# Transposing x of two more blocks by DMA, and a planner that expects later landings

## The chip, the cores and the metric

The kernel runs on one core of one Trainium2 chip. The metric is the device time of one execution in microseconds; the median of six runs of the kernel before is 218.59 us (218.05 to 218.89).

## The reference

Attention with a band and a few global keys, and behind it a two-layer feed-forward network with softplus. B = 4 batches, H = 8 heads, S = 768 positions, D = 64; the band holds the 96 positions up to the query, and the first 8 keys of a batch are seen by all queries.

```
scores = q @ k.T / sqrt(D) + bias            # bias = -slope of the head * distance
a      = softmax(where(local or global, scores, -1e9))
x      = (a @ v), heads side by side: 3072 tokens x 512
h      = x @ w_in                             # 512 x 2048
out    = softplus(h) @ w_out                  # 2048 x 512, float32
```

## The kernel before

**Tiling.** The 3072 tokens are 24 blocks of 128, six per batch. Loads of q, k and v come in windows of two blocks (12 windows, number w; block n belongs to window n // 2). The feed-forward network works in groups of 256 tokens, so group g needs blocks 2g and 2g + 1 and no others.

**A block of attention**, in two halves of four heads: scores on TensorE (L488) into one of two PSUM tiles s_ps; for blocks 4 and later VectorE adds the bias and writes z (L519); ScalarE takes the exponential and writes the probabilities pb (L525); TensorE multiplies them with v into the PSUM tile x_ps, of which there is one (P·V, L540 and L543), where a column of ones gives the sum of each row; VectorE takes the reciprocal (L554) and writes the normalized x as xs in bf16 (L555). The second half's P·V waits until that has emptied x_ps. A block needs its own keys and values and those of the block before it in its batch; small copies put the global keys and values in (L457 on GpSimd, L466 on VectorE).

**x transposed.** The feed-forward network wants x with features on the partitions, in the tile XT. There are two ways, chosen by the constant X_DMA. Blocks below it: four PE transposes against the identity (x_transp, L565) into a PSUM bank and one copy by VectorE or ScalarE (x_out, L574). Blocks from it on: one DMA transpose of 128x512 issued by SP (x_dma, L577).

**q and k transposed.** Windows below T_DMA = 4 go through TensorE. From window 4 on, q is cast to bf16 by VectorE (L388), k by GpSimd in four pieces (L397), and SP issues two DMA transposes for each (L436). v is cast by GpSimd too (L397, four pieces).

**The feed-forward network.** A unit of the first layer is eight matmuls (mm1, L587) into one of two PSUM banks h_ps; ScalarE takes exp (L598) and, for two units at once, log(1 + e) (L606). There are eight units to a group and twelve groups. The second layer (mm2, L615, and L640 for the last group) accumulates in o_ps, for group 0 in s_ps; VectorE copies it out (L659) and SP stores it (L664).

**What sets the order.** Every engine runs its instructions in the order in which they were emitted. This order comes from a planner (class Planner), which simulates the engines while the program is built: each operation has a duration, operations that it comes after, buffers that it takes and frees, and a rank. An engine that is free takes, of the operations that can start, the one of lowest rank. Ranks come from the block or group, from BASE (a number per block, for the first 14 blocks) and from RANKS (a correction for one operation by its name: pv51.0 is the P·V of block 5, second half). For DMAs the planner keeps a model of the queues; an operation with slack is held to be done that much later than its modelled landing (`self.at(op.end + op.slack, ...)`), which touches the plan and no instruction. When TensorE has nothing to do in the first 24 us of the plan, a filler matmul on zeros is emitted (L727).

**Loads.** All loads of q, k and v are issued by SP in one chain; the weights are issued by GpSimd. A load named in HALVED is issued as two DMAs of four heads each; the cast that follows waits for both.

Of the kernel before, what the change touches and what calls it, by code (L numbers as in the profile page):

```python
# [14 lines left out]


RANKS = {
    "Ck3.0": 26.1, "biasA.0": -5.4, "castv1.1": 16.6, "mm1_1_7.0": -3.8, "mm1_1_6.0": -1.5,
    "mm1_1_4.0": 19.1, "bias71.0": 48.3, "mm2_1_7.0": -15.1, "pv51.0": 12.5, "pv60.0": -32.7,
    "mm2_1_3.0": -38.9, "mm1_0_2.0": 5.1, "mm2_1_5.0": 4.5, "bias20.0": 20.2, "castv4.2": 18.4,  # L20
    "mm1_0_7.0": 13.1, "castv4.0": -15.4, "TX0.0": -16.5, "bias30.0": 6.3, "mm2_1_1.0": 13.7,
    "scores7.0": 10.3, "pv10.0": 15.2, "mm1_2_3.0": -4.2, "mm2_0_3.0": 15.3, "mm1_0_3.0": 18.1,
    "castv4.1": 7.7, "mm1_2_4.0": -12.6, "bias01.0": -7.6, "castv0.3": -1.4, "norm11.0": -4.2,
    "castv0.6": -4.6, "exp61.0": -5.6, "scores50.0": -15.4, "castv3.3": -1.5, "mm2_0_1.0": 16.5,
    "castv2.1": -4.7, "norm20.0": 5.2, "castk5.3": 11.8, "castk4.1": -4.2, "castv0.0": 5.4,
    "mm1_0_4.0": 9.3, "Fq1.0": -2.3, "norm10.0": 6.1, "castv0.5": -0.8, "castv2.2": -0.7,
    "castv3.0": -2.8, "bias0.1": -5.2, "castv1.0": 0.2, "castv3.2": -0.4, "Fk3out.0": -10.8,
    "TX5.0": -6.6,
}
HALVED = "q9 k9 q10 k10 v10 q11 k11 v11".split()  # L30
EARLY, MERGED, T_DMA, X_DMA = 4, 6, 4, 6
SP_ORDER = "Q01 K01 v0a Q23 K23 v0b v1 q2@in1 k2 v2 q3@in2 k3 v3"
POOL_ORDER = "in0@Q23 in1 out0 out1@q2 in2 in3 out2 out3"
BASE = (-29.92, -34.26, -30.09, -12.77, -7.13, 15.38, 14.34, -22.2, 17.37, 24.12, 29.7, 32.51, 31.67, 35.31)


class Op:
# [202 lines left out]
def kernel(  # L240
# [101 lines left out]
    def load(w, what, heads=slice(0, H), key=None, waits=()):  # L342
        b, ww = divmod(w, WPB)
        src = {"q": q, "k": k, "v": v}[what][b, heads, W * ww : W * ww + W, :]
        dst = raw_of(what, w)[:, heads, :]
        send(key, nc.sync.dma_start(dst, src.rearrange("h (p r) d -> p h (r d)", r=2)), waits)  # L346
# [38 lines left out]
    def cast(eng, w, what, hs=slice(0, H)):  # L385
        src = raw_of(what, w)
        t = tile_of(qkv, (what + "b", w), [P, 2, H, D], BF16)
        copy_on[eng](t[:, :, hs, :], src[:, hs, :].rearrange("p h (r d) -> p r h d", r=2))  # L388

    def cast_by_block(eng, w, what, blk, r, hs=slice(0, H)):  # L390

        if what == "v":
            dst = vb_ring[w % NRING][:, blk, :, 0:D]
        else:
            dst = tile_of(qkv, (what + "b", w), [P, 2, H, D], BF16)[:, blk, :, :]
        src = raw_of(what, w)[64 * blk : 64 * blk + 64, hs, r * D : r * D + D]
        copy_on[eng](dst[64 * r : 64 * r + 64, hs, :], src)  # L397

    def tr_bank(taken):
        return bank_of(taken[-1]).bitcast(BF16)  # L400
# [33 lines left out]
    def transp_dma(w, what, i):  # L434
        dst = q_tile(w) if what == "q" else k_tile(w)
        nc.sync.dma_start_transpose(  # L436
            dst[:, i, :, :], state[what + "b", w][:, i, :, :].rearrange("p h d -> p (h d)")
        )
# [265 lines left out]
    bias0 = const.tile([P, 2, 4, P], BF16, name="bias0")  # L704
    biasA = const.tile([P, 2, 8, P], BF16, name="biasA")
# [36 lines left out]
    def base(n):  # L742
        return BASE[n] if n < len(BASE) else 4.0 * n - 13.0

# [4 lines left out]
    def add_load(w, what, rank, after=(), hs=ALL, key=None, waits=()):  # L749
        nonlocal chain  # L750
        f = 0.5 if hs != ALL else 1.0
        dur, dma = 0.55 * f + 0.05, (64 * f, 28)
        takes = ((what + "32",),) if hs.start == 0 else ()
        o = chain = pl.add(
            f"load{what}{w}", "sp", dur, lambda op: load(w, what, hs, key, waits), rank,
            after=[*after, *(landed[x] for x in waits)], behind=[chain], takes=takes, dma=dma,
        )
        loaded.setdefault((w, what), []).append(o)
        return o
# [13 lines left out]
    def load_rest(w, rank, after=()):  # L773
        for i, what in enumerate("qkv"):
            for hs, _ in halves if what + str(w) in HALVED else whole:
                add_load(w, what, rank + 0.01 * i, after, hs)
# [85 lines left out]
    def attention_window(w):  # L862
# [7 lines left out]
        for part, (hs, ms) in enumerate(whole if w >= 2 else ()):  # L870
            f = len(ms) / NPAIR
            for what in "qk":
                if w < 4:
                    eng = {"pool": 1.05 * f, "act": 0.2 + 0.85 * f, "dve": 0.1 + 0.6 * f}
                else:
                    eng = {"dve": 0.69} if what == "q" else {"pool": 1.05}
                if what == "k" and w >= T_DMA:
                    c = [
                        pl.add(
                            f"castk{w}", {"pool": 0.68}, 0,  # L880
                            lambda op, blk=blk, r=r: cast_by_block(op.on, w, "k", blk, r),
                            u - 7.93 + 0.01 * blk, after=loaded[w, "k"],
                            takes=(("kb",),) if blk == r == 0 else (),
                        )
                        for blk in range(2) for r in range(2)
                    ]
                    for x in c[1:]:
                        x.behind.append(c[0])
                        x.left += 1
                    pl.add(  # L890
                        f"k{w}", "none", 0.0, lambda op: None, -999.0, after=c,
                        frees=[(loaded[w, "k"][0], "k32")],
                    )
                    casts[w, "k", 0] = c[0]
                else:
                    c = casts[w, what, part] = pl.add(
                        f"cast{what}{w}", eng, 0,
                        lambda op, what=what, hs=hs: cast(op.on, w, what, hs),
                        u - (7.94 if w < T_DMA else 5.33) + 0.1 * (what == "k"),
                        after=loaded[w, what],  # L900
                        takes=((what + "b",),),
                        frees=[(loaded[w, what][0], what + "32")],
                    )
                    c = [c]
                wait = [*c, *(done if what == "k" else ())]
                takes = (("qT",),) if what == "q" else ()
                free_b = [(casts[w, what, 0], what + "b")]
                r = u + (-3.8 if what == "q" else -2.3)
                if w >= T_DMA:
                    for i in range(2):  # L910
                        o = pl.add(
                            f"D{what}{w}", "sp", 1.3,
                            lambda op, what=what, i=i: transp_dma(w, what, i), u - 14.96,
                            after=wait if what == "q" else [*c[2 * i : 2 * i + 2], *done],
                            takes=takes if i == 0 else (), dma=(32, 27), slack=1.2,
                            frees=free_b if i else (),
                        )
                        outs.setdefault((w, what, 0), []).append(o)
                        if i == 0:
                            first_t[w, what] = o  # L920
                    continue
                t = pl.add(
                    f"T{what}{w}", "pe", 0.45 * f,
                    lambda op, what=what, ms=ms: transp(w, what, tr_bank(op.taken), ms),
                    r, after=wait, takes=(*takes, TR),
                )
                first_t[w, what] = t
                o = pl.add(
                    f"T{what}{w}out", {"dve": 0.28 + 0.42 * f, "act": 0.2 + 0.8 * f}, 0,
                    lambda op, t=t, what=what, ms=ms: transp_out(  # L930
                        op.on, w, what, tr_bank(t.taken), ms
                    ),
                    r + 0.1, after=[t], frees=[(t, TR_ALL), *free_b],
                )
                outs[w, what, part] = [o]
        split = w < 2 and f"v{w}a" in landed
        for part, (hs, _) in enumerate(halves if split else whole):
            f = 0.5 if split else 1.0
# [134 lines left out]
    for w in range(NWIN):  # L1073
        attention_window(w)
        for n in (2 * w, 2 * w + 1):
            attention_block(n)

    mm1s, mm2s, lns, copies = {}, {}, {}, {}
    for g in range(NGRP):
# [18 lines left out]
        if g == NGRP - 1:  # L1098
            before = None
            for part, (ns, cols, _) in enumerate(LAST):  # L1100
                f = (cols.stop - cols.start) / DM
# [97 lines left out]
```

## Time and profile before

| | |
|---|---|
| median of six runs | 218.59 us |
| the profiled execution | 218.67 us |
| its span, first to last instruction | 216.9 us |
| TensorE matmul (PE) busy | 208.7 us, 96% |
| ScalarE (ACT) busy | 154.2 us, 71% |
| VectorE (DVE) busy | 121.7 us, 56% |
| GpSimd (POOL) busy | 58.0 us, 27% |
| DMA queue of SP, share of 16 engines | 60.3% |
| L587 matmuls, first layer | 768, 95.9 us busy |
| L615 matmuls, second layer | 295 recorded, 75.3 us busy |
| L565 PE transposes of x | 24 (20 into h_ps, 4 into o_ps) |
| L577 DMA transposes of x | 18, median 3.0 us from issue to landing |
| granted TensorE clock | 1.000 |

Busy times of matmuls overlap, because they are pipelined: four transposes of 219 ns each take 0.39 us together. Starts are recorded and ends are modelled, so a distance from start to start is the safer measure of what one costs. The page cuts the span into 40 slices of 5.4 us; a digit is the busy share in tenths. In the lists of time, "idle before" in square brackets is the time that the engine stood before an instruction, and the name behind the arrow is what it waited for. PEld is the loading of weights into TensorE, which runs beside the matmuls. Some matmul records are missing.

### The profile page before, as it was taken

To read this page: it belongs to the slowest core of one execution; us is meant where nothing else is said; L and a number is where in the kernel's file an instruction comes from. 1 tells how busy PE (TensorE), PEld (TensorE's weight loads), DVE (VectorE), ACT (ScalarE), POOL (GpSimd) and SP (SyncE) were. 2 spreads that over 40 slices of the span, in tenths; PEclk is the share of its full clock that TensorE was granted. 3 is DMA by queue.
4 is the path that set the end of the run, shared out by engine and by line. 5 is a ranking of instruction groups with operands and counts; after the bars stand their busy time and mean duration, and the time that the engine had idled before them with its cause. 6 is when DMAs were issued, how large, how long until landed. Compare 5 with 4: busy or idle time off the path is not lost.

```text
span 216.9 us, 5058 instructions
## 1 busy us (share of the span) xinstructions
PE 208.7 (96%) x2033; PEld 146.2 (67%) x2064; DVE 121.7 (56%) x262; ACT 154.2 (71%) x204; POOL 58.0 (27%) x113
## 2 busy tenths in 40 slices
PE   8799999999899999899999999999999999999994
PEld 7666867776657667577767667667766766676643
DVE  6879686268876657772654854643953753110020
ACT  3666979783788689868769669759669669756630
POOL 4642440015800580440314260314504000000000
PEclk9999999999999999999999999999999999999999
DMA  5999999999965996998687695749764211200112
GB/s 186 327 226 200 248 192 191 260 292 291 137 167 132 292 276 133 294 111 203 159 168 225 141 192 159 195 97 306 175 94 145 74 27 48 76 27 22 51 48 97
DMA packets 70583, 36.24 MB, mean 167 GB/s; under 512 B 28448, under 2 KB 67616, under 8 KB 70560
## 3 DMA queue, kind: packets, MB, share of 16 engines
q1 hardware_dynamic: 66192, 31.53, 60.3%
q0 software_dynamic: 4224, 4.19, 11.9%
q8 instruction: 16, 0.26, 0.5%
q10 hardware_dynamic: 144, 0.20, 0.3%
q14 instruction: 7, 0.06, 0.1%
HBM read 27.26 MB, written 6.29 MB: 155 GB/s over the span
## 4 chain that ended last, share of the span: by engine, by line
PE 66%; DMA 16%; SPq 5%; DVE 4%; ACT 3%; POOL 2%; issue 2%; DVEq 0%; POOLq 0%
PE h_ps L587 28%; PE o_ps L615 25%; DMA q<-in_q_dram 13%; PE s_ps L488 4%; DMA k<-in_k_dram 3%; PE x_ps L543 3%; PE s_ps L640 3%; SPq L346 2%; SPq L436 2%; POOL kb L397 1%; POOL vb L397 1%; ACT e L598 1%; ACT g L606 1%; DVE xs L555 1%; PE s_ps L615 1%
## 5 line engine op out<-in xcount | busy, mean ns | idle before, releaser
L587 PE MATMUL h_ps<-XT,w_in_bf 128*128 128x256 bf16 x768 | 95.9, 273 | 0.1
L598 ACT ACTIVATE e<-h_ps 128x512 f32<-128x512 f32 x96 | 58.6, 630 | 38.7 <-PE h_ps L587 38.2
L587 PEld LDWEIGHTS <-w_in_bf 128*128 128x128 bf16 x768 | 73.1, 98 | 19.3
L615 PE MATMUL o_ps<-w_out_bf,g 128*128 128x512 bf16 x295 | 75.3, 379 | 1.4 <-issue 0.2
L606 ACT ACTIVATE g<-e 128x1024 bf16<-128x1024 f32 x48 | 50.5, 1054 | 0.7
L615 PEld LDWEIGHTS <-g 128*128 128x128 bf16 x352 | 32.2, 98 | 26.7
L525 ACT ACTIVATE pb<-z 128x1024 bf16<-128x1024 f32 (+1 forms) x40 | 39.5, 987 | 6.9 <-DVE z L519 6.5
L519 DVE TENSOR_TENSOR z<-s_ps,biasA 128x1024 f32<-128x1024 f32 x34 | 40.7, 1219 | 6.3 <-PE s_ps L488 4.7
L397 POOL CAST vb<-v 64x512 bf16<-64x512 f32 (+1 forms) x40 | 24.8, 620 | 36.6 <-DMA v<-in_v_dram 32.4
L554 DVE RECIPROCAL rcp<-x_ps 128x4 f32<-128x4 f32 x47 | 8.5, 180 | 36.1 <-PE x_ps L543 33.7
L397 POOL CAST kb<-k 64x512 bf16<-64x512 f32 x32 | 19.6, 612 | 26.9 <-DMA k<-in_k_dram 16.0
L659 DVE COPY osb<-o_ps 128x512 f32<-128x512 f32 x20 | 13.7, 686 | 21.7 <-PE o_ps L615 21.6
L555 DVE TENSOR_TENSOR xs<-x_ps,rcp 128x256 bf16<-128x256 f32 x47 | 19.9, 424 | 1.7
L543 PEld LDWEIGHTS <-pb 128*128 128x128 bf16 x320 | 14.6, 97 | 3.3 <-issue 0.7
L543 PE MATMUL x_ps<-vb,pb 128*128 128x65 bf16 x312 | 15.8, 193 | 0.8 <-DVE xs L555 0.6
L388 DVE CAST qb<-q 128x1024 bf16<-128x1024 f32 x10 | 7.1, 710 | 13.7 <-DMA q<-in_q_dram 13.7
L488 PEld LDWEIGHTS <-kT 64*128 64x128 bf16 x288 | 8.3, 94 | 7.1 <-issue 6.5
L488 PE MATMUL s_ps<-qT,kT 64*128 64x128 bf16 x288 | 12.2, 218 | 0.0
L457 POOL COPY kT<-kT 128x32 bf16<-128x32 bf16 x12 | 2.9, 239 | 31.0 <-PE s_ps L488 24.2
L727 PE MATMUL o_ps<-zeros 128*128 128x128 bf16 x88 | 9.3, 259 | 1.4 <-DVE zeros L682 1.0
L466 DVE COPY vb<-vb 4x512 bf16<-4x512 bf16 (+1 forms) x36 | 10.1, 280 | 0.6
L529 ACT ACTIVATE pb<-s_ps 128x1024 bf16<-128x1024 f32 (+1 forms) x8 | 7.3, 917 | 2.7 <-PE s_ps L488 2.7
(77 smaller groups left out, 101.7 us busy)
## 6 DMA issues: line engine op xcount, KB each, us to landing
out_dram<-osb SPq DMA_DIRECT2D x23, 256.0 KB, 2.4
q<-in_q_dram SPq DMA_DIRECT2D x9, 512.0 KB, 6.2
k<-in_k_dram SPq DMA_DIRECT2D x9, 512.0 KB, 7.2
v<-in_v_dram SPq DMA_DIRECT2D x9, 512.0 KB, 5.9
w_in_bf<-in_moe_w_in_dram POOLq DMA_DIRECT2D x4, 512.0 KB, 8.8
w_out_bf<-in_moe_w_out_dram POOLq DMA_DIRECT2D x4, 512.0 KB, 11.4
v<-in_v_dram SPq DMA_DIRECT2D x6, 256.0 KB, 4.0
q<-in_q_dram SPq DMA_DIRECT2D x6, 256.0 KB, 3.7
```

What stands on the lines that cost most here:

```text
L397: copy_on[eng](dst[64 * r : 64 * r + 64, hs, :], src)
L466: nc.vector.tensor_copy(vb_of(n - 1)[sl, hs, 0:D], vb_of(first)[sl, hs, 0:D])
L488: nc.tensor.matmul(s_t[:, 4 * sub + (lh // 2 if i == 0 else 2 * (lh // 2) + b), :], k_of(n - b, rows, m), q_of(n, rows, m), start=begin, s ...
L519: nc.vector.tensor_tensor(packed(n, z), rows_of(n, s_t), bias, ALU.add)
L525: nc.scalar.activation(pb[:, 0:nr, :], z[:, 0:nr, :], AF.Exp, scale=1.0 / root_d)
L543: nc.tensor.matmul(xv[:, lh, :], pb[:, 2 * j + b, :], vb_of(n - b)[:, h, :], start=b == 0, stop=b == 1,)
L555: nc.vector.tensor_tensor(xs[:, 4 * half : 4 * half + 4, :], xv[:, :, 0:D], rcp[:][:, :, None].to_broadcast([P, 4, D]), ALU.mult,)
L587: nc.tensor.matmul(hv[:, j, :], w_in_bf[:, m, fb * P : fb * P + P], XT[:, m, W * g : W * g + W], start=(m == 0), stop=(m == NM - 1),)
L598: nc.scalar.activation(e[:, p % 2, :].rearrange("p (a t r) -> p a r t", a=4, r=2), state["h", g, p][:].rearrange("p (a r t) -> p a r t", a ...
L606: nc.scalar.activation(gt[:, 4 * c : 4 * c + 4, :].rearrange("p a t -> p (a t)"), state["e", g, c][:].rearrange("p a t -> p (a t)"), AF.Ln ...
L615: nc.tensor.matmul(dst, state["g", g][:, fb, ns * P : ns * P + P], w_out_bf[:, fb, :], start=(fb == 0), stop=(fb == NFB - 1),)
L659: copy_on[eng](osb[:], src)
```

## The change

Three constants, one argument and one dictionary:

```diff
-HALVED = "q9 k9 q10 k10 v10 q11 k11 v11".split()
-EARLY, MERGED, T_DMA, X_DMA = 4, 6, 4, 6
+HALVED = "q10 k10 v10 q11 k11 v11".split()
+EARLY, MERGED, T_DMA, X_DMA = 4, 6, 4, 4
...
-BASE = (-29.92, -34.26, -30.09, -12.77, -7.13, 15.38, 14.34, -22.2, 17.37, 24.12, 29.7, 32.51, 31.67, 35.31)
+BASE = (-34.16, -41.89, -26.9, -10.31, -16.35, 4.3, -5.52, -6.96, 17.37, 24.12, 29.7, 32.51, 31.67, 35.31)
...
         o = chain = pl.add(
             f"load{what}{w}", "sp", dur, lambda op: load(w, what, hs, key, waits), rank,
             after=[*after, *(landed[x] for x in waits)], behind=[chain], takes=takes, dma=dma,
+            slack=2.0 if w >= 4 else 0.0,
         )
...
                         pl.add(
-                            f"castk{w}", {"pool": 0.68}, 0,
+                            f"castk{w}",
+                            {"pool": 0.68, "dve": 0.42, "act": 0.62} if w < 4 else {"pool": 0.68}, 0,
                             lambda op, blk=blk, r=r: cast_by_block(op.on, w, "k", blk, r),
```

X_DMA goes from 6 to 4: x of blocks 4 and 5 is transposed by SP's DMA instead of TensorE. The planner takes loads of windows 4 to 11 to be done 2.0 us later than modelled. q and k of window 9 are loaded in one DMA each. The last edit stands inside `if what == "k" and w >= T_DMA`, with T_DMA = 4.

The table RANKS is a new one, of 40 entries instead of 51. Of its old entries, these bear on the blocks and units that the prediction speaks of (old, new; a dash where there is none):

| operation | old | new |
|---|---|---|
| scores50.0 | -15.4 | -9.99 |
| pv51.0 | 12.5 | - |
| mm1_0_2.0, mm1_0_3.0 | 5.1, 18.1 | 12.71, 15.36 |
| mm1_0_4.0, mm1_0_7.0 | 9.3, 13.1 | -, 19.83 |
| mm1_1_2.0, mm1_1_3.0, mm1_1_4.0 | -, -, 19.1 | -2.58, -23.05, 20.88 |
| mm1_2_0.0, mm1_2_3.0, mm1_2_4.0 | -, -4.2, -12.6 | 4.16, 3.38, -12.5 |

With constants and ranks changed, the order of emission changes on every engine.

## The prediction

> **What bounds the kernel now.** I read the page's slices first, then busy time by stretches, then what TensorE (PE) waited for, then the order of time around each wait. Of the page:
>
> ```profile
> span 216.9 us, 5058 instructions
> ...
> PE   8799999999899999899999999999999999999994
> ...
> DMA  5999999999965996998687695749764211200112
> ```
>
> PE is at nine tenths almost everywhere, and the DMA engines are at nine for the first quarter of the span. So after the start the time is PE's work plus whatever PE waits. The stretches say how much that is (columns: stretch and its length, then busy us and instructions of PE, PEld, DVE, ACT, POOL, clock, DMA share, GB/s):
>
> ```profile
> 8.00:24.00 16.00, 15.30 (x229) 11.69 (x231) 12.68 (x39) 11.12 (x15) 5.99 (x13) 1.00 1.14 247
> 24.00:34.00 10.00, 9.89 (x104) 6.83 (x104) 6.87 (x12) 8.48 (x13) 4.90 (x7) 1.00 1.11 198
> 34.00:57.00 23.00, 22.21 (x219) 16.06 (x221) 15.13 (x29) 15.99 (x23) 6.22 (x11) 1.00 1.21 252
> 57.00:100.00 43.00, 42.02 (x432) 29.24 (x437) 29.94 (x61) 35.04 (x45) 15.91 (x28) 1.00 0.92 197
> 100.00:164.00 64.00, 63.42 (x604) 44.01 (x614) 36.56 (x66) 48.15 (x65) 18.67 (x35) 1.00 0.73 176
> ```
>
> PE lacks 0.79 us in 34 to 57 and 0.98 in 57 to 100, and the list of PE's waits has just two entries of note after 24 us:
>
> ```profile
> PE x_ps L540 <- DVE xs L555: 0.6, 1, 0.6
> PE x_ps L543 <- DVE xs L555: 0.6, 1, 0.6
> ```
>
> Both are P·V matmuls that want the one bank x_ps, which VectorE (DVE) has not yet emptied. The timeline tells why. First wait:
>
> ```profile
> 53.64 0.29 PE L540 MATMUL x_ps<-vb,pb 128*128 128x65 bf16 x4
> ...
> 54.62 0.85 DVE L388 CAST qb<-q 128x1024 bf16<-128x1024 f32 x1 [1.22 <-DMA q<-in_q_dram]
> ...
> 55.39 0.16 DVE L554 RECIPROCAL rcp<-x_ps 128x4 f32<-128x4 f32 x1
> ...
> 55.59 0.42 DVE L555 TENSOR_TENSOR xs<-x_ps,rcp 128x256 bf16<-128x256 f32 x1
> ...
> 56.06 0.29 PE L540 MATMUL x_ps<-vb,pb 128*128 128x65 bf16 x4 [0.60 <-DVE xs L555]
> 56.06 0.16 PEld L540 LDWEIGHTS <-pb 128*128 128x128 bf16 x3 [0.77 <-issue]
> ```
>
> The first P·V was done at 53.93, but the next instruction on DVE was a cast of q whose load landed only at 54.59. DVE stood 1.22 us, the normalization queued behind the cast came late, and PE with it. Second wait, the same pattern:
>
> ```profile
> 87.78 0.69 DVE L388 CAST qb<-q 128x1024 bf16<-128x1024 f32 x1 [0.96 <-DMA q<-in_q_dram]
> ...
> 88.60 0.42 DVE L555 TENSOR_TENSOR xs<-x_ps,rcp 128x256 bf16<-128x256 f32 x1
> ...
> 89.08 0.40 PE L543 MATMUL x_ps<-vb,pb 128*128 128x65 bf16 x8 [0.55 <-DVE xs L555]
> 89.08 0.28 PEld L543 LDWEIGHTS <-pb 128*128 128x128 bf16 x7 [0.73 <-issue]
> ```
>
> **Part 1: no PE transposes for blocks 4 and 5.** Eight matmuls of L565 and two copies (L574) go. Four transposes take PE from one start to the next 47.78 - 47.56 = 0.22 us, and PE has no slack there, so two blocks give **-0.44 us**. The copies were ACT's, at 38.49 (0.58) and 48.09 (0.56); ACT then stood 2.80 us before its next exponential, so they are worth nothing.
>
> Two DMA transposes come in their place, on SP's queue. Each of the 18 that are there takes SP about 1.22 us to issue and lands after 2.4 to 4.8 us. SP is never free from 34 to 57 us, but there it waits for room in a full queue: eight loads in a row land about 1.8 us apart. So the DMA time counts. Transposes in a full queue land 0.45 to 0.66 us apart (80.12, 80.57, 81.06, 81.72), hence all loads behind the two come 0.9 to 1.3 us later. I cost that at nothing: k of window 4 (landed 51.01) gives kT at 59.64 and its scores start at 61.97, 2.3 us of cover; q of window 5 was cast by 55.5 and its transposes were issued at 60.82, 5.3 us of cover. Without that cover it is 0.9 to 1.3 us. The xs buffers of the two blocks are held until the transposes land; there are three, so a third block can go on.
>
> The question is when x of block 5 lands. PE's timeline, columns start and length:
>
> ```profile
> 45.13 0.41 PE L543 MATMUL x_ps<-vb,pb 128*128 128x65 bf16 x8
> ...
> 47.56 0.39 PE L565 MATMUL h_ps<-ident,xs 128*128 128x128 bf16 x4
> ...
> 50.37 1.04 PE L587 MATMUL h_ps<-XT,w_in_bf 128*128 128x256 bf16 x8
> ```
>
> Two groups have 16 units of eight L587 matmuls, and 16 had been issued by 46.25. The 17th, at 50.37, is therefore the first of group 2, which needs blocks 4 and 5. Loads issued by SP between 39.59 and 47.22 took 7.4 to 9.6 us to land. A transpose of block 5 sent where its normalization ends now (46.92) would land with q of window 5, at 54.6: too late. But block 5's last P·V stands at 45.13 only because of the order (its rank carries +12.5): its probabilities were ready at 40.03 (exponential at 38.96, 1.07 us) and x_ps was free at 39.22. The new table has no such entry and ranks block 5 at 4.3 instead of 15.38. With P·V at 40.1 the normalization ends near 41, the transpose goes out just behind q of window 4, which landed at 49.21, and lands near 49.7, 0.7 us in time. I take no cost, with 0 and the slower rival's 3.2 us as ends.
>
> The Trainium skill speaks against this part: "VectorE: DVE Perf Modes", sections "The three transpose paths" and "Rules for kernel authors", lists 390 ns for a 128x128 transpose by TensorE against 1309 ns by DMA, and advises TensorE where PSUM will do as the destination. By its figure eight transposes would be 3.1 us of PE, and the sum below 2.7 us lower; the trace has them pipelined at 0.22 us for four, and that is what I use.
>
> **Part 2: slack.** It emits no instruction. The planner believes loads of windows 4 and later 2.0 us later, so it queues other work ahead of the casts. Both waits above were a cast at the head of DVE's queue, 1.22 and 0.96 us before its data; both are under 2.0. With normalization first, the P·V of 56.06 could have gone at 55.3 and that of 89.08 at 88.35. I price the waits by PEld's idle time, because starts are recorded and matmul ends modelled: 0.77 + 0.73 = **-1.50 us** (by PE's idle time 0.60 + 0.55 = 1.15, the other end). What is late next is the cast, by the 0.6 us of reciprocal and multiply; the 5.3 us above cover that.
>
> **Part 3: small edits.** q9 and k9 are no longer loaded by halves: their casts wait for both halves anyway, and PE has no wait over 0.1 us from 100 to 164. Nothing; if that cover went, a half, 0.9 us (landings 119.04 and 119.93). The options for castk need w < 4 inside a branch for w >= 4: never taken.
>
> **Part 4: the new order.** This the trace can't show. Six casts of q waited on their loads here and two of them cost PE something, though this order too was planned against landing times. I charge one new wait of that size: **+0.75 us**, ends 0 and 1.50 (both back). The start is open as well: 49 fillers (L727) of about 0.056 us from one start to the next, 2.7 us, stand in 8 to 24 us. A better order could put work there, a worse one add as many: -2.7 to +2.7. I take 0, since the same loads with the same order of transfers feed it.
>
> **Sum.** Against the profiled execution, 218.67 us (216.9 of span and 1.77 around it): 218.67 - 0.44 - 1.50 + 0.75 = 217.48. The median, 218.59, lies 0.08 lower: **217.4 us**.
>
> **Rivals.** *Block 5's x lands late* (slower). If its P·V stays behind other work, the transpose lands at 54.6 instead of by 50.37, and PE has no first-layer unit left. It would have 1.0 us of other work (scores at 51.34 and 53.86, P·V at 53.64), so it stands 54.6 - 50.4 - 1.0 = 3.2 us, in the place of the 0.75 charged in part 4: 217.4 - 0.75 + 3.2 = 219.85, say 219.9. It turns the change slower than before once the landing is later than 50.4 + 1.0 + 1.94 (the gains), near 53.3. For it: 7.4 to 9.6 us in the queue. Against: the 5 us by which block 5 can move up. *The waits only move* (no change): slack shifts an order, and DVE again stands ahead of a normalization twice; only the 0.44 us of the transposes are left: 218.15, at the edge of what can be told. For it: DVE has 29.94 us of work in the 43 us from 57 to 100, with few holes. *Nothing new goes wrong* (faster): no new wait, 216.65; with a third of the fillers filled, 0.9 us, 215.75.
>
> **Numbers.** Forecast 0.42; late landing 0.30; waits only move 0.15; nothing goes wrong 0.13. About 0.2%, 0.44 us, is what a measurement can tell from no change. Faster: forecast and the last, 0.55. Same: 0.15. Slower: 0.30. Range: 215.8, the last rival with its fillers, to 219.9, the late landing; beyond it remain a worse start or a later landing, about 2 in 10. Range of the forecast alone: 216.65 to 218.15.
>
> **What would show it.** Right: no L565 for blocks 4 and 5 (16 matmuls left of 24), 20 transposes at L577, no PE wait on DVE xs with an L388 just ahead, the 17th unit of L587 by about 50 us. Wrong: a hole in PE near 50 us ended by an XT landing; new waits between 57 and 100 us; more fillers before 24 us.

## The result, and the profile after

The changed kernel takes **220.52 us** (median of 21 runs, 219.05 to 221.95) where the kernel before takes 218.6 (47 runs beside it): a ratio of 1.0093, 95% interval 1.0075 to 1.011. It is 1.9 us slower; the forecast was 1.2 us faster. Where single executions of a run fell in a slower state (one of a_noentry, three of b_x4), the times here leave them out. The profiled execution took 220.83 us. Its page, the lines that answer to those shown of before:

```profile
span 219.1 us, 5036 instructions
...
PE   7799999999999969999999999999999999999994
...
DMA  6999999999969976997964995895964211400112
```

PE's row has one new dent, the 6 in the fifteenth slice (77 to 82 us). The stretches of the changed kernel (stretch and length, busy us and instructions of PE, PEld, DVE, ACT, POOL, then clock, DMA share, GB/s; the DMA share is the time of all packets over that of 16 engines, and can pass 1):

```profile
34.00:57.00 23.00, 22.67 (x214) 15.61 (x217) 15.18 (x27) 16.63 (x23) 4.61 (x8) 1.00 1.18 246
57.00:75.00 18.00, 17.84 (x188) 12.55 (x189) 12.41 (x24) 14.32 (x19) 7.67 (x14) 1.00 1.04 208
75.00:79.50 4.50, 2.69 (x30) 1.81 (x29) 2.43 (x6) 2.10 (x3) 3.61 (x6) 1.00 1.27 212
79.50:83.00 3.50, 3.36 (x13) 1.82 (x12) 2.01 (x2) 1.56 (x2) 1.62 (x4) 0.51 0.55 110
83.00:100.00 17.00, 16.79 (x193) 12.35 (x195) 12.16 (x25) 14.61 (x21) 5.06 (x9) 1.00 0.98 183
```

From 34 to 57 PE now lacks 0.33 us instead of 0.79, and from 83 to 100 us 0.21 instead of 0.82 (before had 16.18 busy of those 17 us): both old waits are gone from this trace. All of the loss is in 75 to 83 us. PE idles 1.81 us of the first 4.5, and in the next 3.5 it is "busy" with 13 instructions, because its clock is granted at 0.51: 3.5 x 0.49 = 1.7 us of clock. The list of PE's waits names what ended the idle time:

```profile
PE s_ps L485 <- DMA qT<-qb: 1.0, 1, 1.0
...
PE o_ps L612 <- DVE osb L656: 0.8, 1, 0.8
```

PE's timeline there, and after it SyncE's queue (start, length):

```profile
75.81 0.93 PE L584 MATMUL h_ps<-XT,w_in_bf 128*128 128x256 bf16 x7
77.78 0.63 PE L485 MATMUL s_ps<-qT,kT 64*128 64x128 bf16 x16 [1.04 <-DMA qT<-qb]
79.18 1.57 PE L612 MATMUL o_ps<-w_out_bf,g 128*128 128x512 bf16 x3 [0.77 <-DVE osb L656]
80.55 1.91 PE L584 MATMUL h_ps<-XT,w_in_bf 128*128 128x256 bf16 x8
82.25 1.36 PE L612 MATMUL o_ps<-w_out_bf,g 128*128 128x512 bf16 x4
```

```profile
68.00 0.58 SPq L343 DMA_DIRECT2D q<-in_q_dram  x1
68.63 0.57 SPq L343 DMA_DIRECT2D k<-in_k_dram  x1
69.25 1.26 SPq L343 DMA_DIRECT2D v<-in_v_dram  x1
70.55 3.81 SPq L433 DMA_TRANSPOSE qT<-qb  x1
```

The scores of block 10 wait for the second transpose of q of window 5 (the name Dq5.0 in the plan). It stands in the queue behind the three loads of window 6, which land at 72.29, 75.57 and 77.36; it lands at 77.74, and PE starts 0.04 us later. In the kernel before the same two transposes were issued at 60.82 and 62.10, ahead of those loads. The output copy on DVE (L656) then waits for a store that landed at 78.34, still to free its buffer, and PE for that copy. The 80.55 group shows the clock: eight first-layer matmuls take 82.25 - 80.55 = 1.70 us, where 0.87 is usual.

**A reading used from here on: the lag.** In a trace the useful work of PE is counted by its weight loads (each at its own streaming time); the time at which the same amount of work is reached in two kernels tells where one falls behind. Against before, the changed kernel is 0.4 us late at 25 us, level at 50, **0.4 to 1.1 ahead between 57 and 70** (the two orders differ, so it swings), 0.61 ahead at 75, and **2.88 late at 83**: 3.5 us lost in eight. It wins 0.71 back at 88 (the old second wait) and ends 2.15 late.

### The profile page after: what moved, and what is told of

Read it like the earlier page. It is cut to its first block, busy times and chain, and to the rows that moved or that the text cites. A ratio compares the mean times of both kernels' runs of the same rounds, so it can differ in the third digit from the quotient of the medians.

```text
span 219.1 us, 5036 instructions
## 1 busy us (share of the span) xinstructions
PE 209.5 (96%) x2023; PEld 146.2 (67%) x2056; DVE 123.0 (56%) x260; ACT 153.3 (70%) x203; POOL 58.8 (27%) x114
## 4 chain that ended last, share of the span: by engine, by line
PE 73%; DMA 10%; DVE 8%; SPq 4%; ACT 2%; issue 2%; POOL 0%; POOLq 0%
PE h_ps L584 33%; PE o_ps L612 26%; DMA v<-in_v_dram 6%; PE s_ps L485 4%; PE x_ps L540 4%; DMA qT<-qb 3%; PE s_ps L637 3%; SPq L343 2%; SPq L433 2%; DVE vb L394 1%; ACT e L595 1%; DVE osb L656 1%; PE s_ps L612 1%; DVE biasA L721 1%; PE o_ps L724 1%
## 5 line engine op out<-in xcount | busy, mean ns | idle before, releaser
L394 POOL CAST kb<-k 64x512 bf16<-64x512 f32 x32 | 20.6, 645 | 33.4 <-DMA k<-in_k_dram 32.1
L656 DVE COPY osb<-o_ps 128x512 f32<-128x512 f32 x20 | 13.7, 685 | 25.0 <-PE o_ps L612 23.1
L463 DVE COPY vb<-vb 4x512 bf16<-4x512 bf16 (+1 forms) x36 | 12.1, 335 | 0.5
L724 PEld LDWEIGHTS <-zeros 128*128 128x128 bf16 x88 | 7.2, 117 | 2.0 <-DVE zeros L679 1.0
```

Of the source, the lines that this page charges most:

```text
L656: copy_on[eng](osb[:], src)
L724: nc.tensor.matmul(o_ps[:, 0:P], zeros[:], zeros[:])
```

## The experiments

Three theories. **A, one place:** the order puts Dq5.0 behind three loads (its new RANKS entry is +6.4); moved back, all is well. **B, the queue:** the two added DMA transposes make a full queue later by more than the work behind it can bear; where the lateness shows is chance. **C, the slack:** emptying the old waits only shifts them. Edits of the order move one finished instruction of the plan behind another, without planning anew, by a helper that the diffs below call:

```
def put(key, behind):
    keys = [getattr(op, "key", "") for op in plan]
    op = plan.pop(keys.index(key))
    keys.remove(key)
    plan.insert(keys.index(behind) + 1, op)
```

Labels with a_ start from the changed kernel, with b_ from the kernel before. Ratios are against the kernel before on the same chip (medians 218.6 to 219.0), with 95% intervals.

### A: one place

**a_dq5**

```diff
+    put("Dq5.0", "Dq5.1")
```

> The changed kernel with one instruction moved: the second DMA transpose of q of window 5 (Dq5.0) is issued directly behind its sibling (Dq5.1) and not behind the loads of q, k and v of window 6; every other order is kept. Theory (one place in SP's queue makes the loss): the transpose lands near 66 us instead of 77.74, block 10's scores start near 76.6 without a wait, PE's work is never more than 0.3 us behind the changed kernel's before 75 us and some 3 us ahead after 83 us: 217.2 to 217.9, that is 2.6 to 3.3 us under the changed kernel and 0.7 to 1.4 under the kernel before. Rival 1 (two more transposes make the loaded queue late, wherever one of them stands): another transpose or load lands late and PE waits about as long elsewhere: 220 to 221. Rival 2 (the order of VectorE, made for later landings, is the cost): no change, 220 to 221.

220.93 us, ratio 1.0107 (1.0077 to 1.0137): nothing gained. qT now lands at 65.88 and PE no longer waits for it, but other waits stand in its place, each on a transfer. Two of them on DVE's timeline:

```profile
75.05 0.69 DVE L385 CAST qb<-q 128x1024 bf16<-128x1024 f32 x1 [1.96 <-DMA q<-in_q_dram]
...
79.24 0.69 DVE L656 COPY osb<-o_ps 128x512 f32<-128x512 f32 x1 [0.94 <-DMA out_dram<-osb]
```

PE stands 0.78 us until 69.73 (first layer on XT of block 7, now behind a load), 0.73 until 76.34 (behind that cast) and 0.94 until 79.98 (behind that copy); by the lag each costs some 0.9 to 1.1 us. Theory A falls: the place moved, the loss stayed.

**a_noentry** plans the changed kernel anew without the entry.

```diff
-    "mm1_2_4.0": -12.5, "castv0.1": -0.11, "Dq5.0": 6.4, "Dq4.0": 0.49, "mm1_2_2.0": -8.92,
+    "mm1_2_4.0": -12.5, "castv0.1": -0.11, "Dq4.0": 0.49, "mm1_2_2.0": -8.92,
```

> The changed kernel without the entry Dq5.0 (+6.4) in RANKS, planned anew; the order is the same up to the loads of window 5 and differs in some 50 places of PE's order behind it. Theory: as with the transpose moved by hand, 217.2 to 217.9; the later differences are worth 0.3 us either way. Rivals 1 and 2: 220 to 221.

221.95 us, 1.0145 (1.0097 to 1.0193). The new plan has one wait of 3.0 us from 78.7, on the output copy. Four of its six executions show a mean clock of 0.985 to 0.992, so part of this time is a fall of the clock; the profiled one (220.84 us) has none and is no faster than the changed kernel either. Again not the entry.

**b_dq5** is the converse: the delayed place alone, in the kernel before.

```diff
+    put("Dq5.0", "loadv6.0")
```

> The converse: the kernel before with its first DMA transpose of q of window 5 moved on SP behind the loads of k and v of window 6; nothing else moves, block 4's and 5's x still go through PE. Theory: the transpose is issued near 74 us and lands near 79 to 80 us, block 10's scores, now at 77.28, wait 2 to 3 us, and the slower clock after such a wait may add: 220.5 to 222. Rival 1 (it takes the two more transposes): 218.3 to 219.0. Rival 2 (it takes the changed order of VectorE): 218.3 to 219.0.

219.68 us, 1.0053 (1.0034 to 1.0073), +1.1 us, with a PE wait of 1.7 us on qT at 79. So the place does cost something where all else is as before, but less than the whole and less than had been expected.

**a_fix1** and **a_fix2** move whatever was late in a_dq5 up as well.

```diff
+    put("Dq5.0", "Dq5.1")
+    put("loadv5.0", "Dk5.1")
+    put("store1_0.0", "Dk5.1")
```

> The changed kernel with three instructions of SP moved: the late transpose of q of window 5 directly behind its sibling, the first store of group 1 and the load of v of window 5 directly behind k's transposes of window 5, so that all three stand ahead of the loads of q, k and v of window 6. Everything else keeps its order. Theory (not one place but the queue: whatever stands behind a run of loads between 57 and 82 us lands late, and a transpose, an XT, a store that frees an output buffer all stood there): PE's waits on XT (0.94 us lost) and on the output copy (1.12) of the run with the transpose alone moved go, the cast of q of window 6 still blocks VectorE (0.90): 218.6 to 219.6. Rival (two more transposes make this stretch late, and it paces PE in any order): the waits move to other landings, 220.3 to 221.5.

223.66 us, 1.0218 (1.0166 to 1.0269), the slowest of all: the load of q of window 6 became later still (it lands at 76.54, in a_dq5 at 75.03), and the cast of q in front of a normalization cost PE 3.6 us until 77.9. The clock fell as well, to 0.50 for 6.8 us from 76.86, 5.8 of them with PE at work, which is another 2.9 us. All six executions show a fall (mean clock 0.985 or 0.992, here 0.985), so most of the 3.1 us over the changed kernel is clock. a_fix2 takes the casts out of that place too:

```diff
+    put("castq6.0", "gv10.0")
+    put("Dq6.0", "castq6.0")
+    put("Dq6.1", "Dq6.0")
+    put("castq7.0", "norm110.0")
```

> As the run before it in this list, and on VectorE the cast of q of window 6 moved behind both normalizations of block 9 and the copies behind them, with its two transposes behind it in the order of emission (their place on SP stays), and the cast of q of window 7 behind the normalization of block 11's first half. Theory (queue): all four waits between 57 and 100 us are gone: 217.0 to 217.9, under the kernel before. Rival (the stretch paces PE in any order): 219.5 or more.

221.27 us, 1.011 (1.0073 to 1.0147). The 3.6 us went, 2.1 us of waits for kT came (the global-key copy follows a cast that is late too), and 1.3 on output copies. Whatever is sent earlier makes something else later: that points to a queue that is short of time and not to an order, which the next runs test.

### B: the transposes' DMA time

**b_2t** adds to the kernel before nothing but two DMA transposes of 128 KB, of weights into tiles that nobody reads, behind the load of v of window 3, where the change has its own two.

```diff
+    spare = [const.tile([P, NPAIR, P], BF16, name=f"spare{i}") for i in range(2)]
     for op in plan:
         op.fn(op)
+        if getattr(op, "key", "") == "loadv3.0":
+            for t in spare:
+                nc.sync.dma_start_transpose(t[:], w_in_bf[:, 0, 0:DM])
```

> The kernel before with two DMA transposes of 128x512 added on SP behind the load of v of window 3, from a weight tile into two spare tiles that nothing reads; no work is left out and no order changes. It measures what two more transposes cost in the full queue, without what they save. My step in the prediction: the loads behind them land 0.9 to 1.3 us later, covered by 2.3 and 5.3 us, time unchanged, 218.3 to 218.9. Rival (transposes among loads hold the queue longer than their spacing tells, and the stretch paces PE): loads 1.5 to 2.5 us later, 219.3 to 221.

**221.71 us, 1.0141 (1.009 to 1.0193): +2.7 us from the two transfers alone.** The two land at 47.81 and 48.31, 0.5 us apart, as the prediction had it. Behind them q of window 4 lands at 50.34 (before 49.21), q of window 5 at 56.11 (54.59), and twenty-five microseconds on k of window 6 is still late, 77.69 (75.83). By then PE itself is 1.4 us behind (the lag, level from 58 to 88 us), so this later lateness is the whole kernel's and not the queue's alone. PE and DVE where it shows first:

```profile
52.31 0.29 PE L488 MATMUL s_ps<-qT,kT 64*128 64x128 bf16 x4 [0.74 <-DVE osb L659]
...
57.47 0.29 PE L540 MATMUL x_ps<-vb,pb 128*128 128x65 bf16 x4 [1.36 <-DVE xs L555]
```

```profile
50.36 0.69 DVE L388 CAST qb<-q 128x1024 bf16<-128x1024 f32 x1 [0.63 <-DMA q<-in_q_dram]
...
56.14 0.73 DVE L388 CAST qb<-q 128x1024 bf16<-128x1024 f32 x1 [2.09 <-DMA q<-in_q_dram]
```

The cast at 56.14 is the one of the prediction's first wait: it stood 1.22 us there and stands 2.09 here, and PE's 0.60 became 1.36. The cast at 50.36 is a new wait of the same kind. DVE takes its instructions in order, so a late q holds up the normalizations and output copies behind the cast at once; it doesn't first use up the margin until q's own scores.

**b_2t_late** has the same two behind the last load of v (near 160 us).

```diff
+        if getattr(op, "key", "") == "loadv11.1":
```

> The kernel before with the same two added DMA transposes into spare tiles, now behind the last load of v, near 160 us, where the DMA share is 0.27 and less. Theory (what two transposes cost is the place in the full queue ahead of the loads of windows 4 and 5, whose casts stand in VectorE's line): no cost, 218.4 to 219.0. Rival (a transpose costs by itself, by SP's issue time or otherwise, wherever it stands): 1 us or more over the kernel before.

219.07 us, 1.0009 (0.998 to 1.0037): no cost. The two land at 166.29 and 167.04; the DMA share from 163 to 168 us is 0.60 with them and 0.44 in the kernel before, and no load of q, k or v stands behind them. So neither the instructions nor the bytes cost anything as such; the early place does. Whether by its full queue or by the loads that stand behind, this run alone doesn't part.

**b_2copy** puts plain copies of the same bytes in the first place.

```diff
+                nc.sync.dma_start(t[:].rearrange("p m t -> p (m t)"), w_in_bf[:, 0, 0:DM])
```

> The kernel before with two plain DMA copies of the same 128 KB each, from the same weight tile into the same spare tiles, in the place of the two added transposes behind the load of v of window 3. It tells bytes from the way of moving them. If the cost is queue time in proportion to bytes: loads of window 4 about 0.9 to 1.1 us later as with the transposes, 220.5 to 221.7. If it is the transposes: loads less than 0.6 us later, 218.5 to 219.7.

220.5 us, 1.0068 (1.0037 to 1.0098): +1.5. They land 0.40 us apart, and q of window 4 lands at 49.59, 0.38 late against 1.13 with the transposes; the expectation's two halves came apart, the load as in its second case and the time as in its first. Counted from the load of v of window 3 to that of q of window 4, the two take 0.78 us as copies and 1.21 as transposes. By the medians more than half of b_2t's price is what any transfer of this size costs there; the other 1.2 us would be the transposing (the two intervals just overlap). The Trainium skill, "Advanced Engine Details and Errata", section "X-Bar Transpose (TRN2)", says that transpose DMAs are as fast as regular ones, at about 90% of a copy's bandwidth. The spacing of landings, 0.40 against 0.50, is not far from it; the kernel's time, +1.5 against +2.7, is.

**a_nodx** goes the other way: the changed kernel in its order, without the two transfers.

```diff
     def x_dma(n):
+        if n < 6:
+            nc.gpsimd.tensor_copy(
+                XT[:, :, P * n : P * n + P],
+                state["xs", n][:].rearrange("p (m a) d -> p m (a d)", a=2),
+            )
+            return
```

> The changed kernel, its order kept, without the two DMA transposes of x of blocks 4 and 5: in their place in the program GpSimd copies xs into XT (128x512 bf16, twice), so x of these two blocks is not transposed and that part of the computation is changed. GpSimd was idle there. Theory (the loss is the DMA time of the two transposes in the full queue): loads of windows 4 and 5 land 1 to 2 us earlier than in the changed kernel, the transpose of q of window 5 lands before 76.5, and the time falls to 217.5 to 218.9. Rival (the new order is at fault with or without them): 219.8 or more.

**218.63 us, 0.9995 (0.9971 to 1.002): 1.9 us less than the changed kernel** (2.1 by the two ratios, since they ran on different chips). The whole loss against before is gone with them, though Dq5.0 still stands behind three loads. The two copies on GpSimd take 0.62 us each; they bring x of these blocks earlier than a transpose would, but the changed kernel's PE didn't wait for that x (under "Right" below).

**after_2** and **a_nodx_2** are second traces of the changed kernel and of a_nodx, unaltered, on one chip: the first trace of the changed kernel had the fall of the clock, which the clocks of 19 of its 21 timed runs don't show (0.998 or more; the median of these 19 is 220.42 us, so the clock is not the loss).

> The changed kernel unaltered, for a second trace: the first one caught a fall of TensorE's granted clock to 0.50 behind its hole (79 to 83 us, (1 - clock) summed is 1.70 us), which the clocks of 18 of its 21 runs do not show. Theory (the DMA time of the two transposes): without that fall the loads of windows 4 to 6 still land 0.8 to 1.9 us later than in the kernel whose x of blocks 4 and 5 is copied by GpSimd, TensorE still waits between 70 and 85 us on qT, xs or osb for 1.5 to 3 us, and the time is 219.5 to 221. Rival (the clock): without the fall the holes of 70 to 85 us are under 1.2 us and the time is below 219.4.

> The kernel that copies x of blocks 4 and 5 by GpSimd without transposing it (the output of those blocks is not the reference's), for a second trace beside the second one of the changed kernel: its first profiled execution, 219.55 us, was among its longest (median 218.63). Theory: holes between 70 and 85 us of 0 to 1.0 us, time 218.2 to 219. Rival (the clock alone separates the two): the same holes as the changed kernel without its fall, time within 0.5 us of it.

219.38 and 218.07 us, one execution each, both with the clock at 1.00 throughout. after_2 is at the lower end of its kernel's runs, under the range expected of it and at the edge of what the rival (the clock alone) allowed; the holes decide. PE of after_2:

```profile
77.89 0.63 PE L485 MATMUL s_ps<-qT,kT 64*128 64x128 bf16 x16 [0.77 <-DMA qT<-qb]
79.30 1.02 PE L612 MATMUL o_ps<-w_out_bf,g 128*128 128x512 bf16 x3 [0.78 <-DVE osb L656]
80.16 1.04 PE L584 MATMUL h_ps<-XT,w_in_bf 128*128 128x256 bf16 x8
81.03 1.03 PE L612 MATMUL o_ps<-w_out_bf,g 128*128 128x512 bf16 x4
```

and of a_nodx_2:

```profile
76.35 0.63 PE L485 MATMUL s_ps<-qT,kT 64*128 64x128 bf16 x16
77.80 1.02 PE L618 MATMUL o_ps<-w_out_bf,g 128*128 128x512 bf16 x3 [0.82 <-DVE osb L662]
```

The two waits of the first trace are there again without any fall of the clock, and without the two transposes the one on qT is gone. The loads of window 6 land at 72.44, 75.67 and 77.47 with them, at 71.09, 74.12 and 75.80 without. after_2 falls 0.41 us behind a_nodx_2 at 50 to 54, 0.37 at 70 (a first-layer group waits for XT) and 0.70 at 76: 1.50 in all, none of it clock. These are single executions, both at the low end of their kernels. The first trace of a_nodx (219.55 us, median 218.63) waits 0.13 us for qT instead of not at all, and ends level with after_2, because it loses 0.9 us at 89 on a wait that the others don't have (below, part 2). So the traces show where the transposes tell, and the medians what they cost. In the first trace the fall came on top: 2.15 us late against before there, 0.59 in after_2, 1.56 between them beside the 1.7 us of clock.

### C: slack and casts

**b_casts** takes the two old waits away and changes nothing else.

```diff
+    put("castq5.0", "norm60.0")
+    put("castq7.0", "norm110.0")
```

> The kernel before with two casts of q moved on VectorE: that of window 5 behind the normalization of block 6's first half, that of window 7 behind that of block 10's or 11's first half (norm60 and norm110), each one place later; nothing else moves. Theory (my step that priced the two waits at 1.50 us): both PE waits go and the time falls by 1.2 to 1.5 us: 217.1 to 217.4. Rival (the waits only move on, since the casts are late then): less than 0.5 us gained, 218.1 or more.

218.88 us, 1.0028 (1.0001 to 1.0055): no gain. Both waits are gone (the lag falls by 0.76 and 0.71 at their places), and 0.46, 0.33 and 0.58 us come back at 77, 89 and 107. The first of these on DVE:

```profile
76.77 0.69 DVE L659 COPY osb<-o_ps 128x512 f32<-128x512 f32 x1 [1.07 <-DMA out_dram<-osb]
```

PE arrives earlier and waits for a store instead: the transfers came no sooner.

**b_slack** is the kernel before with the slack alone, planned anew.

```diff
             after=[*after, *(landed[x] for x in waits)], behind=[chain], takes=takes, dma=dma,
+            slack=2.0 if w >= 4 else 0.0,
```

> The kernel before with the slack of 2.0 us on loads of windows 4 and later alone, planned anew with its own RANKS and BASE; block 4's and 5's x still go through PE. My step in the prediction: both waits of P·V on a blocked VectorE go, 217.1 to 217.5. By the run with the two casts moved by hand (no gain, three other waits of 0.3 to 0.6 us in their place): 218.2 to 219.2.

219.33 us, 1.0032 (1.0002 to 1.0062). Both old waits gone; one of 1.8 us at 78, again an output copy behind a store.

**b_2t_casts** is b_2t with the casts of q of windows 4, 5 and 7 moved behind what they held up.

```diff
+    put("castq4.0", "oc1_0.0")
+    put("Dq4.0", "castq4.0")
+    put("Dq4.1", "Dq4.0")
+    put("castq5.0", "norm60.0")
+    put("castq7.0", "norm110.0")
```

> The kernel before with the two added transposes behind the load of v of window 3, and with three casts of q moved on VectorE: that of window 4 behind three output copies, that of window 5 behind the normalization of block 6's first half, that of window 7 behind that of block 11's first half. Theory (the lateness reaches PE through the casts in VectorE's line): the waits of 0.93, 1.53 and 0.99 us of the run without the moves go, the time falls from 221.7 by 1.5 to 3: 218.7 to 220.2. Rival (the inputs themselves come too late for PE): 221 or more.

221.1 us, 1.0099 (1.0065 to 1.0132): 0.6 under b_2t. The waits at 51, 55 and 90 went; by the lag 1.4 us at 57.6 (P·V, now waiting for later probabilities) and 0.7 to 0.8 at 78, 90 and 109 came. The casts are how lateness reaches PE first, not why it does.

### Better versions, and other settings

**b_best** is b_casts with output buffers of their own, five of them, so that no copy waits for a store. **a_best** does the same to the changed kernel, with its late transposes and casts moved.

```diff
+    outs_pool = ctx.enter_context(tc.tile_pool(name="outs", bufs=5))
...
-        osb = tile_of(ffn, ("osb", g, ns), [P, DM], F32)
+        osb = tile_of(outs_pool, ("osb", g, ns), [P, DM], F32)
```

> The kernel before with the two casts of q moved as in the first run of that kind, and with five buffers for the output copies in place of three (own pool; the planner still counts three, so the order is the same). Theory (what came back there, 0.46, 0.33 and 0.58 us, were output copies waiting for stores to land): those go and the 1.3 to 1.5 us of the two repaired waits stay gained: 217.1 to 217.8. Rival (they wait for something else): 218.5 to 219.2 as before.

> The changed kernel with the late transpose of q of window 5 moved behind its sibling, the load of v of window 5 behind the transpose of x of block 7, the casts of q of windows 6 and 7 behind normalizations on VectorE, and five output buffers. Each of the waits seen in the run with the transpose alone moved (0.94 on XT, 0.90 on xs, 1.12 on the output copy) has its cause taken away. Theory: 217.3 to 218.5. Rival (the queue is late by as much as the two transposes hold it and some other landing ends PE's waits): 219.5 or more.

b_best: 219.07 us, 0.9999 (0.9971 to 1.0026). The store waits are gone and PE still waits three times, 1.4 us in all, for the output copy: now that stands behind casts of q whose loads are late. a_best (Dq5.0 behind Dq5.1, v of window 5 behind the x of block 7, casts of windows 6 and 7 behind other work): 219.56 us, 1.0026 (1.0005 to 1.0048). That is 1.0 less than the changed kernel (1.5 by the ratios) and still not below the one before. No version beat the kernel before.

**b_x4** and **b_x8** set X_DMA to 4 and 8 in the kernel before and plan it anew with its old tables.

```diff
-EARLY, MERGED, T_DMA, X_DMA = 4, 6, 4, 6
+EARLY, MERGED, T_DMA, X_DMA = 4, 6, 4, 4
```

> The kernel before with X_DMA = 4 alone, planned anew with its own RANKS and BASE (made for 6): block 4's and 5's x by DMA. Theory: the 2.7 us that two added transposes cost, less the 0.44 us of PE, and block 5's P.V is still ranked late, so its x lands late for group 2 as well: 221 to 224. My step in the prediction with x landing in time: 218.2.

> The other direction: the kernel before with X_DMA = 8, planned anew with its own RANKS and BASE: x of blocks 6 and 7 through PE too, two transposes fewer on SP between 58 and 66 us. Theory: 0.44 us of PE are paid, the loads and transposes behind come about 1 us earlier, and a wait or two goes: 217.5 to 219.0. Rival (PE's work is all that counts): 219.0 to 219.6.

b_x4: 223.13 us, 1.0192 (1.0141 to 1.0244); its trace is of an execution of 225.95 us and is read for its clock alone (last section). b_x8, with two transposes fewer than before: 220.76 us, 1.0086 (1.0053 to 1.0118), off both expectations, with waits of 1.6 us on XT and 1.3 on exponentials. Ranks searched for one setting don't seem to carry to another, so these two say nothing on the price of a transpose.

## Why the prediction was wrong

**The step that failed** is in part 1: "hence all loads behind the two come 0.9 to 1.3 us later. I cost that at nothing: ... 2.3 us of cover ... 5.3 us of cover." The lateness was about right (in b_2t 1.1 us at the next load and 1.5 at q of window 5). Its price is not nothing but 1.9 us (medians of the changed kernel and a_nodx; 1.5 between the traces of after_2 and a_nodx_2) or 2.7 (b_2t, in the old order). The cover failed twice over. It was the margin between a load and its own scores, while the cast in front of it in DVE's line passes the lateness on at once. And it was read from the old order: the new one sent the transposes of q of window 5, whose 5.3 us were counted on, behind three more loads, and used it up itself.

**Part 2, -1.50, was given back, and half of it was not earned by the order.** At the first place the new order does put the cast behind the normalization. At the second it does not: the cast of q of window 7 still stands right ahead of it on DVE (at 89.74 and 90.34 in the changed kernel). In the first trace of a_nodx, which has the same order, the old wait is back, on DVE and on PE:

```profile
88.38 0.69 DVE L385 CAST qb<-q 128x1024 bf16<-128x1024 f32 x1 [1.09 <-DMA q<-in_q_dram]
88.99 0.18 DVE L551 RECIPROCAL rcp<-x_ps 128x4 f32<-128x4 f32 x1
...
89.67 0.40 PE L540 MATMUL x_ps<-vb,pb 128*128 128x65 bf16 x8 [0.68 <-DVE xs L552]
```

That the changed kernel's two traces lack it is luck: the load happened to land before DVE came to the cast. Both waits went in b_casts and b_slack too; neither got faster. The prediction named the casts as next in line and gave them cover; it did not see that from 50 to 110 us stores and loads arrive only just in time, so that what PE had won was lost again to the next of them, 0.3 to 0.6 us at a time in b_casts.

**Part 4** charged one new wait of 0.75. The first trace has two new ones, 1.04 and 0.77, and a fall of the clock of 1.7 us behind them. The second of the two is the new order's own: it stands in a_nodx (0.84) and a_nodx_2 (0.82) as well. The new waits between 57 and 100 us are one of the signs that the prediction named for being wrong.

**The sum again.** Forecast 217.4. The changed kernel without its two transfers is at 218.6: 1.2 of the gains did not come. With them 220.5: 1.9 more. The forecast's terms without a DMA term were thus off by 1.2 us, and the missing term was the larger error.

**Right:** the transposes gone from PE (16 L562 left, 20 L574), no PE wait on xs behind a cast in 34 to 57 (at 88 by luck, as said); 47 fillers from 8 to 24 us where 49 were; and x of block 5, on which the slower rival hung: its transpose landed at 48.71 and the seventeenth first-layer unit started at 51.05, so group 2 did not wait. The time went to the slower side by another mechanism than that rival's. "The waits only move" had its part right (b_casts), for a reason not given there, and priced the transposes' DMA at nothing as well.

**Open.** Which of the late transfers PE meets differs from plan to plan and somewhat from run to run; a rule for it was not found. Why transposes cost more than copies of the same bytes is only narrowed down (last section), and no run has an empty queue with loads behind the two. Not tried: the two transposes issued from another engine's queue.

## What to carry to other kernels

An engine at 96% can still be paced by transfers in one stretch: before moving work from it to a DMA queue, look whether that stretch's queue is full (here SP free at no time from 34 to 57 us, DMA share 1.2) and price the transfer at its queue time on the path, unless the new order, not the old, shows the cover. A cast in an in-order engine passes a late load on to all that stands behind it, and a wait removed ahead of a stretch that transfers pace is given back within it. Two cheap tests went furthest here: add the transfer alone, reading nothing, in the full place and in an empty one; and take it out of the changed kernel, order kept.

## What the hardware showed that was not expected

- **Queues held up where transposes meet loads.** In the changed kernel DMA throughput falls to 18 GB/s from 76 to 77 us, with a load, two transposes and two stores outstanding; k of window 6 lands 3.28 us behind q (75.57, 72.29), where 1.8 is usual (3.03 in a_nodx_2, so this one comes with the new order). By the durations of packets, some 8 to 24 at a time take 1.4 to 2.4 us at such places: at 54.6 and 57.0 in before, at 45.2, 58.6 and 75.4 in the changed kernel. Kernels with the added transposes at 40 to 44 us have one near 45; the others have not. The queue moves 24 GB/s from 46.2 to 47.4 us in the changed kernel against 294 in a_nodx, and 18 from 46 to 47 in b_2t against 292 in b_2copy: a likely part of what transposes cost beyond copies, though not tested by itself. What holds the packets was not found.
- **The clock fell to 0.50 for 3.41 us** (from 79.51) behind two idle times of 1.04 and 0.77 us, 0.6 us apart, in the changed kernel's first trace, and not in after_2 behind nearly the same two (0.77 and 0.78), nor in a_noentry's behind one of 2.99. In b_x4 it fell for 3.41 us behind 1.01 and 0.91, 0.3 us apart, and again for 3.41 behind one of 3.40; in a_fix1 for twice as long, 6.83 us, beginning 2.5 us into an idle time of 3.55. The Trainium skill, "TensorE: Matmul & The Clock Gate", section "HAM oscillation — how this bites in real kernels", gives as the rule no idle gaps over some 3.4 us; the one of the changed kernel and the first of b_x4 came behind shorter ones.
